# Sparse attention in front of a gated MLP: visits of four units over a DRAM image, filler matmuls in the front, a new order

## The chip, the core and the metric

One core of one Trainium2 chip runs the whole program. The metric is the device time of one execution in microseconds (us); the number given for a kernel is the median of its runs.

## What is computed

The program joins two operators. The first is attention over 8 batches x 8 heads, 576 positions and 64 values per head. Heads 0 to 3 let a query see its own position and the 31 before it; heads 4 to 7 let it see the earlier positions that leave the same remainder by 32. The second is a gated MLP on the 4608 x 512 result.

```python
scores = q @ k.T / sqrt(D)
rel = pos[:, None] - pos[None, :]
mask_local = (rel >= 0) & (rel < 32)                          # heads 0..3
mask_strided = (rel >= 0) & (pos[None] % 32 == pos[:, None] % 32)   # heads 4..7
attn = softmax(where(mask, scores, -1e9)) @ v                 # 8 x 8 x 576 x 64
x = attn.transpose(0, 2, 1, 3).reshape(4608, 512)
xn = x / sqrt(mean(x * x, axis=-1) + 1e-6) * rms_g
g = xn @ w_gate                                               # 512 -> 1536
out = (g * sigmoid(g) * (xn @ w_val)) @ w_out                 # 1536 -> 512
```

## The kernel before

The MLP works on nine chunks of 512 tokens. Each float32 product is made of three matmuls on rounded parts (high x high, low x high, high x low), and the program has 3528 matmuls of 128x512 for them; their lines are L1040, L1119, L1508, L1673, L1897 and L2099. Chunk 0 goes alone and the last two together in their own way (L1508, L1673); chunks 1 and 2 join for their output product (L1897), and chunks 3 to 6 go by pairs in a scheme that saves products (L2099, L1897).

The attention is cut into 96 units: a batch, a pair of heads (`p`; below 2 local, else strided) and a third of the queries (`j`). A unit has one or two tiles per head, of 96 queries (local) or of 108 to 126 queries (strided, by the table `RES`). There are two paths.

- **The old path** (units 0 to 19). Fifteen of these units form the front, which runs before the first large matmul; the others stand between the large matmuls of chunk 0. Steps: scores (in the front over zero-padded copies of the keys, L697, of all 128 rows; else over 64 rows, L701; a mask is added by a bf16 matmul, L691, in the front), row maximum on DVE, four exps on ACT (L728), normalization, transposes on PE with an identity (L796) and a copy (L800), values (L832). Squares and their sums for the RMS factor follow (L897, L902, L929, L948).
- **Visits** (units from `BT` = 20 on). `step_e` and `step_d` make one visit of two units. Scores are matmuls of 32x64 on the band alone (L587), DVE masks and takes the row maximum over 128 columns (L594), ACT makes the exps (L601), DVE the reciprocals (L619, L620), ACT or POOL the normalization (L631, L633). DVE transposes blocks of 32x32 over 1024 columns (L644). Three moves within SBUF of 32 KB each (L647) carry the blocks that belong to the next group of keys, and ACT or POOL clears the place they came from (L651, L653). At a later visit the values follow (L826).

The MLP's weights arrive in an eight-byte form; during chunk 0 ACT, DVE and POOL convert them (L2259 to L2281) and SP stores them to DRAM (L2285, L2288). The RMS factor of chunk 1 onwards is made by a column sum over all 128 partitions (L929 for chunk 1), a square root on ACT with its table load (L979) and four reciprocals on DVE (L982).

What sets the order: each operation is recorded in a `Plan` with an engine, a cost and what it reads and writes. The table `ORDER` (a packed list of numbers) then gives the sequence in which each of the five engines issues, and it is followed as it stands. A DMA issued by SP that must wait holds up all that is behind it on SP. Every instruction of PE that waits holds up PE.

## Time and profile before

| what | us |
|---|---|
| median of 3 runs (lowest, highest) | 949.84 (949.37, 953.02) |
| the profiled execution's own time | 951.61 |
| its span in the profile | 949.8 |
| PE busy / DVE busy / ACT busy / POOL busy | 925.6 / 771.4 / 624.4 / 308.5 |

The mean granted clock of PE in that execution is 0.998 of full speed. A matmul of float32 operands leaves two records in the profile, so "x48" in a timeline row of scores stands for 24 matmuls; a 128x512 matmul of the MLP leaves one. Matmuls overlap in the pipeline, so the price of one is read from start to start; its own duration is longer. "Idle before" is time in which an engine had nothing to do, with what released it.

### The profile page before, as it was taken

The numbers are of one execution on the slowest core, as the hardware profiler recorded it, in microseconds if no ns is written. First come the engines' busy times: TensorE is split into PE (matmuls) and PEld (weight loads), VectorE is DVE, ScalarE is ACT, GpSimd is POOL, SyncE is SP. The second block draws the span as 40 slices with busy tenths as digits, with TensorE's granted clock in tenths as the row PEclk, the third lists the DMA queues.
The fourth block names the chain that finished last, engine by engine and source line by source line (L and its number), as shares of the span: only waits on it lengthen the run. The fifth ranks groups of instructions, "written<-read, shape, count | busy, mean of one in ns | idle before, by whom it ended". The sixth has DMA issues, their size and how long they took to land.

```text
span 949.8 us, 18934 instructions
## 1 busy us (share of the span) xinstructions
PE 925.6 (97%) x6470; PEld 744.4 (78%) x6470; DVE 771.4 (81%) x1810; ACT 624.4 (66%) x1758; POOL 308.5 (32%) x294
## 2 busy tenths in 40 slices
PE   8999999999999899999999999999999999999998
PEld 7777766887788687788887778788888888888886
DVE  5899999978988999988768999755579995467891
ACT  7999996658786789776569786656377633333340
POOL 7334335336334322445212423201034310114130
PEclk9999999999999999999999999999999999999999
DMA  9999666664556677965765779684537794683561
GB/s 298 391 355 387 221 256 229 204 215 167 174 189 221 207 251 259 369 263 182 246 204 170 226 245 357 234 319 154 193 115 216 247 374 177 236 299 130 172 184 66
DMA packets 100928, 223.22 MB, mean 235 GB/s; under 512 B 11552, under 2 KB 34784, under 8 KB 100832
## 3 DMA queue, kind: packets, MB, share of 16 engines
q1 hardware_dynamic: 100064, 221.17, 67.3%
q8 instruction: 51, 0.84, 0.4%
q10 hardware_dynamic: 768, 0.85, 0.3%
q14 instruction: 45, 0.37, 0.1%
HBM read 171.05 MB, written 47.19 MB: 230 GB/s over the span
## 4 chain that ended last, share of the span: by engine, by line
PE 77%; DVE 9%; DMA 6%; ACT 5%; issue 1%; ACTq 0%; SPq 0%; DVEq 0%
PE acc L2099 10%; PE g L2099 6%; PE v L2099 6%; PE acc L1897 6%; PE v L1897 5%; PE g L1040 5%; PE g L1897 5%; PE v L1040 4%; PE acc L1040 4%; PE acc L1508 3%; PE v L1508 3%; PE g L1508 3%; PE acc L1119 2%; PE acc L826 2%; PE pair L587 2%; PE g L1673 2%
## 5 line engine op out<-in xcount | busy, mean ns | idle before, releaser
L1040 PE MATMUL g<-xh,wg 128*128 128x512 f32 x192 | 61.3, 399 | 1.9 <-DVE e L1056 1.4
L1040 PE MATMUL v<-xh,wv 128*128 128x512 f32 x184 | 58.8, 400 | 0.7 <-DVE e L1094 0.7
L601 ACT ACTIVATE pp<-pp,my 96x128 f32<-96x128 f32 (+2 forms) x146 | 56.6, 392 | 3.9 <-DVE my L594 3.9
L919 POOL TENSOR_TENSOR ssq<-ssq,srt 128x512 f32<-128x512 f32 x21 | 28.8, 1369 | 82.8 <-ACT srt L914 82.8
L601 ACT ACTIVATE pT<-pT,my 96x128 f32<-96x128 f32 (+2 forms) x130 | 50.4, 392 | 1.3 <-DVE my L594 1.2
L1040 PEld LDWEIGHTS g<-xh,wg 128*128 128x128 f32 x192 | 34.9, 188 | 11.4 <-DVE e L1056 2.3
L1040 PEld LDWEIGHTS v<-xh,wv 128*128 128x128 f32 x184 | 33.6, 188 | 9.4 <-DVE e L1094 1.0
L1040 PE MATMUL g<-xl,wg 128*128 128x512 f32 x96 | 37.6, 391 | 1.3 <-DVE xl L1015 1.3
L631 ACT ACTIVATE pp<-pp,my 96x128 f32<-96x128 f32 (+2 forms) x118 | 37.0, 391 | 1.2 <-DVE my L620 1.0
L879 ACT COPY raw<-acc 128x192 f32<-128x192 f32 (+16 forms) x97 | 22.2, 345 | 23.1 <-PE acc L826 21.0
L1040 PE MATMUL v<-xl,wv 128*128 128x512 f32 x92 | 36.1, 392 | 0.2 <-DVE xl L1015 0.2
L594 DVE CUSTOM_DVE_ANT_0 pp<-pair,cb 96x128 f32<-96x128 f32 (+2 forms) x146 | 33.1, 282 | 1.8 <-PE pair L587 1.7
L587 PEld LDWEIGHTS pair<-xx,xx 64*32 64x32 f32 (+2 forms) x1920 | 22.2, 105 | 14.9 <-issue 10.4
L651 ACT ACTIVATE pp<-pp 32x256 f32<-32x256 f32 x44 | 18.2, 415 | 23.7 <-DMA pp<-pp 23.1
L1040 PE MATMUL acc<-xh,wv 128*128 128x512 f32 x104 | 32.7, 395 | 0.8 <-DVE or L1086 0.8
L1119 PE MATMUL acc<-or,hh 128*128 128x512 f32 x96 | 30.8, 400 | 1.2 <-POOL or L2281 1.2
L631 ACT ACTIVATE pT<-pT,my 96x128 f32<-96x128 f32 (+2 forms) x96 | 30.0, 397 | 3.0 <-DVE my L620 3.0
L1040 PE MATMUL acc<-xh,wg 128*128 128x512 f32 x96 | 30.3, 397 | 0.3 <-DVE hl L1056 0.2
L594 DVE CUSTOM_DVE_ANT_0 pT<-pair,cb 96x128 f32<-96x128 f32 (+2 forms) x130 | 29.2, 282 | 0.6 <-PE pair L587 0.6
L587 PE MATMUL pair<-xx,xx 64*32 64x64 f32 (+1 forms) x1920 | 28.2, 221 | 1.2 <-DVE pair L579 1.0
L2099 PE MATMUL acc<-wg,wv 128*128 128x512 f32 x102 | 28.7, 390 | 0.0
L2099 PE MATMUL acc<-wv,wv 128*128 128x512 f32 x102 | 28.7, 389 | 0.0
(918 smaller groups left out, 3143.0 us busy)
## 6 DMA issues: line engine op xcount, KB each, us to landing
wv<-wsv SPq DMA_DIRECT2D x36, 512.0 KB, 8.0
wg<-wsg SPq DMA_DIRECT2D x26, 512.0 KB, 8.3
or<-tg SPq DMA_DIRECT2D x22, 512.0 KB, 6.4
th<-tg SPq DMA_DIRECT2D x21, 512.0 KB, 6.1
tl<-tg SPq DMA_DIRECT2D x21, 512.0 KB, 6.0
xx<-in_qT_dram SPq DMA_DIRECT2D x31, 288.0 KB, 5.5
wg<-wos SPq DMA_DIRECT2D x32, 256.0 KB, 3.7
xx<-in_kT_dram SPq DMA_DIRECT2D x28, 288.0 KB, 5.0
```

What stands on the lines that cost most here:

```text
L587: nc.tensor.matmul(out=singles[0][h][g:g + w, o:o + n], lhsT=qt[r, q0 + g:q0 + g + w], rhs=kt[r, k0 + g:k0 + g + n], start=True, stop=True)
L594: nc.vector.tensor_tensor_reduce(out=PX[x][:m, :, g0 + 2 * h + t], in0=sp[h][:, t], in1=mk[t], scale=-0.125, scalar=3.0e38, op0=ALU.add, o ...
L601: nc.scalar.activation(out=v, in_=v, func=AF.Exp, scale=-1.0, bias=mx2[z][:m, u, h, t:t + 1], accum_out=su2_[z][:m, u, h, t, 0:1])
L631: nc.scalar.activation(out=w, in_=w, func=AF.Copy, scale=mx2[z][:m_, y, h, t:t + 1])
L826: nc.tensor.matmul(out=po[64 * h:64 * h + 64, x * 32 * nx:(x + 1) * 32 * nx].rearrange("d (x q) -> d x q", q=32), lhsT=vt_of(vt, p)[:n, h, ...
L879: nc.scalar.copy(out=d, in_=s)
L919: op("Pool", pool(CH), at, lambda e: (nc.vector if e == "DVE" else nc.gpsimd).tensor_tensor(out=ssq, in0=ssq, in1=roots["srt"], op=ALU.add ...
L1040: nc.tensor.matmul(out=out, lhsT=wt[:, w, sl], rhs=xhl[x, kc], start=(kc == 0 and i == 0), stop=(kc == KC - 1 and i == 2))
L1119: nc.tensor.matmul(out=acc[t], lhsT=x[h][:, sl], rhs=wt[:, w], start=(u == 0 and i == 0), stop=(u == NU - 1 and i == 2))
L1508: nc.tensor.matmul(out=banks[bk], lhsT=w, rhs=X[a, k].tile(y), start=start and k == 0 and i == 0, stop=stop and k == 1 and i == 2, skip_gr ...
L1897: nc.tensor.matmul(out=banks[bks[j]], lhsT=w.tile(v, k, j), rhs=x.tile(k, y), start=start and n == 0 and i == 0, stop=stop and n == KT - 1 ...
L2099: nc.tensor.matmul(out=banks[bk], lhsT=w, rhs=xtile(a, k, y), start=start and k == 0 and i == 0, stop=stop and k == 1 and i == 2, skip_gro ...
```

## The change

1. Front. The keys of a unit arrive in one tile for both heads, without the zero-padded copies, and the scores use 64 rows (L707 after; 11 units move to it). The eight clears of 64x608 on POOL go. Three units (3, 6, 9) are "wide": one subtraction on DVE and one exp over all columns on ACT instead of four exps with their sums. Forty filler matmuls of 128x128 (L2258 after), whose result nobody reads, stand on PE in the front. The two warm-up matmuls of 128x512 (L402) stay, later in the order.
2. Visits have four units, that is two pairs, from unit 24 on; units 20 to 23 go to the old path, whose other form (`TP`) goes. Scores, masks, exps and normalization use a compact band of 64 columns; the block transpose covers 512 columns. The matmuls of scores fall from 960 to 912, the blocks of scores from 38 to 19. Runs of attention work between large matmuls fall from 68 to 57.
3. In place of the moves and clears a pair is written to one of two images in DRAM by two DMAs (L662 after, 96 or 128 KB each, 72 in all) and read back by one (L664, 384 or 512 KB, 36 in all). The read lays each block on its diagonal and brings zeros for the rest; `zeros()` clears both images once, with four DMAs of 256 KB at the start.
4. Chunk 1's RMS factor is made on columns, as chunk 0's is: four small matmuls, nine small operations on DVE, a spread by four 128x128 matmuls (L1001 after) and a copy take the place of one 128x512 float32 matmul, the square root and four reciprocals.
5. In the weights' conversion one ACT operation takes a constant instead of a bias tile, and 12 of 36 roundings go from ACT to DVE.
6. `ORDER` is new as a whole.

```diff
@@ constants
-RES = [7, 7, 6, 6, 6]
+RES = [7, 7, 7, 7, 4]
+RC = (1,)
+WIDE = (3, 6, 9)
+FILL = 40
+VIS = ((12, 12.0, 22, (28, 4, 4)), (22, 0.0, 45, (36, 4, 4, 4, 4, 4, 4)), (45, 0.0, 69, (60, 4, 4, 4, 4, 4, 4)), (69, 0.0, 90, (84, 4, 2, 2, 4)))
-BT = 20
-TP = 21
+BT = 24
+TP = 99
-RELX = {12: 0.0, 13: 36000.0, 14: 0.0, 15: 46000.0}
-RELD = {14: 37000.0, 15: 0.0}
+RELX = {}
+RELD = {}
...
@@ ORDER = (...): all of its lines are replaced
...
+    PC = [t[:, 0:CH].rearrange("q (c g k) -> q c g k", c=2, k=32) for t in qs_]
...
-    for x in range(NPB):
-        op("Pool", 1200, -1, lambda x=x: nc.gpsimd.memset(pq[x], 0.0), writes=[("pp", x)])
...
+    def zeros():
+        zz = tbufs[2]
+        op("Pool", 400, -1, lambda: nc.gpsimd.memset(zz, 0.0), writes=[("ts", 1, 1)])
+        for x in range(2):
+            for y in range(2):
+                op("SP", 430, 0, lambda x=x, y=y: nc.sync.dma_start(out=whole_[x][:, CH * y:CH * y + CH], in_=zz),
+                   reads=[("ts", 1, 1)], writes=[("im", x, y)], bytes_=P * 2048, rel=22000.0)
...
+        c0 = 128 * ((i - BT) % 4)
+        sp = [singles[0][h][:m, c0:c0 + 64 * nt].rearrange("q (t x k) -> q t x k", x=2, k=32) for h in range(2)]
+        mk = [cm[:m, 2 if p > 1 else 0 if j == 0 and t == 0 else 1] for t in range(nt)]
...
-            if i == BT:
-                nc.vector.memset(pair_, 0.0)
-            for t, tt_ in enumerate(tl):
-                q0, k0 = (PAD + LQ * tt_, LQ * tt_) if p < 2 else (PAD + NROW * RES0[tt_],) * 2
+            for t, tile_ in enumerate(tl):
+                q0, k0 = (PAD + LQ * tile_, LQ * tile_) if p < 2 else (PAD + NROW * RES0[tile_],) * 2
                 for g in range(0, m, 32):
-                    w, n = min(32, m - g), min(64, P - g)
+                    qe = min(g + 32, m)
                     for h in range(2):
                         r = slice(64 * h, 64 * h + 64)
-                        o = 256 * u + P * t + g
-                        nc.tensor.matmul(out=singles[0][h][g:g + w, o:o + n], lhsT=qt[r, q0 + g:q0 + g + w], rhs=kt[r, k0 + g:k0 + g + n],
-                                         start=True, stop=True)
+                        w = min(64, SW + 32 - k0 - g)
+                        for a, e, k in ((0, w, k0 + g), (w, 64, k0)):
+                            if e > a:
+                                nc.tensor.matmul(out=singles[0][h][g:qe, c0 + 64 * t + a:c0 + 64 * t + e], lhsT=qt[r, q0 + g:q0 + qe],
+                                                 rhs=kt[r, k:k + e - a], start=True, stop=True)
...
-        op("DVE", DVT + 2 * CH / 0.96, 0, lambda: nc.vector.transpose(out=qs_[x], in_=qs_[x]), reads=[], writes=[("pu", x, 0), ("pu", x, 1), ("pp", x)])
-        for y in range(3):
-            near, far = PX[x][32 * y:32 * y + 32, y + 1].rearrange("k g q -> k (g q)"), PX[x][32 * y + 32:32 * y + 64, y].rearrange("k g q -> k (g q)")
-            op("SP", SPMV, 0, lambda near=near, far=far: nc.sync.dma_start(out=far, in_=near), reads=[("pp", x)], writes=[("pd", x, y)], bytes_=32 * 1024)
-
-            def clear(e, near=near):
-                if e == "ACT":
-                    nc.scalar.activation(out=near, in_=near, func=AF.Copy, scale=0.0)
-                else:
-                    nc.gpsimd.memset(near, 0.0)
-            op(CLW[0][0], CLW[0][1], 0, clear, reads=[("pd", x, y)], writes=[("pz", x, y)], also=CLW[1:])
+        near, z = qs_[x][:, 0:CH], x % 2
+        op("DVE", DVT + CH / 0.96, 0, lambda: nc.vector.transpose(out=near, in_=near), reads=[], writes=[("pu", x, 0), ("pu", x, 1), ("pp", x)])
+        w = 3 if wus[i][1] < 2 and wus[i - 1][1] < 2 else 4
+        for c in range(2):
+            n = min(P - 32 * c, 32 * w)
+            op("SP", 600, 0, lambda c=c, n=n: nc.sync.dma_start(out=diag[z][c][0:n // 32], in_=near[0:n, 256 * c:256 * c + 256]),
+               reads=[("pp", x)], writes=[("im", z, c)], bytes_=n * 1024 + 1)
+        op("SP", 430, 0, lambda: nc.sync.dma_start(out=qs_[x][:, 0:256 * w], in_=whole_[z][:, 0:256 * w]), reads=[("im", z, 0), ("im", z, 1)],
+           writes=[("pp", x)], bytes_=P * 1024 * w + 1)
...
-                    if o < KZ:
-                        nc.tensor.matmul(out=sp[h][:, x], lhsT=qt[:, q0:q0 + m],
-                                         rhs=wraw[kz_key(o, h)].bitcast(F32)[:, k0:k0 + n], start=i >= PM,
-                                         stop=i >= PM or x == nt - 1)
-                    else:
-                        nc.tensor.matmul(out=sp[h][:, x], lhsT=qt[r, q0:q0 + m], rhs=kt[r, k0:k0 + n],
-                                         start=i >= PM, stop=i >= PM or x == nt - 1)
...
+        wide = i in WIDE
+
         def rowmax():
+            if wide:
+                for hs, pr in joint(pn):
+                    full = pr[:m, :, 0:nt * n].rearrange("q h (t k) -> q h t k", k=n)
+                    nc.vector.tensor_reduce(out=mx[:, hs], in_=full, axis=AX.X, op=ALU.max, negate=True)
+                    nc.vector.tensor_tensor(out=pv[:, hs], in0=full, in1=mx[:, hs].unsqueeze(3).broadcast_to([m, hs.stop - hs.start, nt, n]), op=ALU.add)
+                return
...
+            if wide:
+                e = buf[:m, 0:2 * nt * n]
+                nc.scalar.activation(out=e, in_=e, func=AF.Exp, scale=0.125)
+                return
...
+        if c in RC:
+            for t in range(4):
+                op("PE", 230, at, lambda t=t: nc.tensor.matmul(out=banks[bk][:, 0:4], lhsT=ssq[:, P * t:P * t + P], rhs=sel[:, 3 - t:7 - t],
+                                                               start=t == 0, stop=t == 3),
+                   reads=["sel", "ssq"], writes=[key] + alias.get(key, []) + ([("S", 0), ("T", 0)] if bk[0] == "b" else []))
...
+        if c not in RC:
+            op("ACT", act(CH) + 90, at, sqrt, reads=["eps", key], writes=["srt"], tab="sqrt")
+        for q in range(0, CH if c not in RC else 0, P):
...
+    for _ in range(FILL):
+        op("PE", 224 + SMD, 0, lambda: nc.tensor.matmul(out=bank["g"][:, 0:P], lhsT=ones, rhs=ebuf[:, 0:P], start=True, stop=True),
+           reads=["ones", "wz", "e"], writes=["g"])
...
-            nc.scalar.activation(out=lo32, in_=top, func=AF.Identity, scale=1.0 / 32, bias=low3)
-        op("ACT", 655, at, last3, reads=["low3"], writes=[wk])
+            nc.scalar.activation(out=lo32, in_=top, func=AF.Copy, scale=1.0 / 32, bias=-31.0 / 64)
+        op("ACT", 562, at, last3, writes=[wk])
...
```

The order shows it at three places. First, PE at the very start (`pair` and `acc` are PSUM, `wg`/`wv` hold the padded keys, `xx` the queries, `cb` the mask). Before:

```order
L402 MATMUL v<-e,ones 128x512 x2
L691 LDWEIGHTS hl_106
L691 MATMUL pair<-cb,hl_106 96x256
L691 LDWEIGHTS hl_106
L691 MATMUL pair<-cb,hl_106 96x256
L697 MATMUL pair<-wg_180,xx_82 96x128
L697 MATMUL pair<-wv_181,xx_82 96x128
L697 MATMUL pair<-wg_180,xx_82 96x128
L697 MATMUL pair<-wv_181,xx_82 96x128
```

After:

```order
L2258 MATMUL g<-e,ones 128x128 x16
L702 LDWEIGHTS hl_109
L702 MATMUL pair<-cb,hl_109 96x256
L702 LDWEIGHTS hl_109
L702 MATMUL pair<-cb,hl_109 96x256
L707 MATMUL pair<-wg_187,xx_83 96x128 x4
L2258 MATMUL g<-e,ones 128x128 x2
```

The warm-up is replaced by sixteen fillers, and the other 24 stand in groups of one to three further on. Second, PE around a visit (`pp` and `pT` hold a pair's weights, `vt` the values of v). Before, among the products of L1897:

```order
L587 MATMUL pair<-xx_83,xx_82 32x64 x6
L587 MATMUL pair<-xx_83,xx_82 12x32 x2
L587 MATMUL pair<-xx_85,xx_84 32x64 x6
L587 MATMUL pair<-xx_85,xx_84 30x32 x2
L587 MATMUL pair<-xx_85,xx_84 32x64 x6
L587 MATMUL pair<-xx_85,xx_84 30x32 x2
L826 MATMUL acc_70<-pp_97,vt_88 64x96 x8
L826 MATMUL acc_70<-pp_98,vt_87 64x128 x8
L1897 MATMUL acc_72<-wg_3961,wg_3613 128x512 x3
L1897 MATMUL acc_72<-wv_3948,wg_3613 128x512 x3
L1897 MATMUL acc_72<-th_3955,wv_3645 128x512 x3
L1897 MATMUL g<-wg_3320,wg_3700 128x512 x3
```

After:

```order
L600 MATMUL pair<-xx_86,xx_85 32x64 x24
L600 MATMUL pair<-xx_84,xx_83 32x64 x6
L600 MATMUL pair<-xx_84,xx_83 30x64 x2
L600 MATMUL pair<-xx_84,xx_83 32x64 x6
L600 MATMUL pair<-xx_84,xx_83 30x64 x2
L600 MATMUL pair<-xx_84,xx_83 32x64 x6
L600 MATMUL pair<-xx_84,xx_83 30x64 x2
L600 MATMUL pair<-xx_84,xx_83 32x64 x6
L600 MATMUL pair<-xx_84,xx_83 30x64 x2
L850 MATMUL acc_71<-pp_98,vt_88 64x96 x8
L850 MATMUL acc_71<-pp_99,vt_88 64x96 x4
L850 MATMUL acc_71<-pp_99,vt_89 64x96 x4
```

A visit now makes the scores of four units in one run and the values of others behind them. Third, SP around the moves. Before:

```order
L647 DMA pT_99<-pT_99 32x256 x3
L2285 DMA wsv_151<-wv_1845 128x1024
L1309 DMA or_1875<-wos_116 128x2x256
L2288 DMA wos_126<-or_1867 256x1x256 x2
L2288 DMA wos_127<-or_1824 256x1x256 x2
L1309 DMA or_1875<-wos_117 128x2x256
L647 DMA pT_100<-pT_100 32x256 x3
L1303 DMA tt<-wos_116 128x2x256
L1273 DMA tg_157<-th_1924 128x1024
L1273 DMA tg_157<-tl_1935 128x1024
```

After:

```order
L662 DMA im_104<-pp_99 3x32x256
L662 DMA im_104<-pp_99 4x32x256
L1353 DMA or_2387<-wos_124 128x2x256
L1315 DMA to_197<-th_1918 512x1x256
L662 DMA im_103<-pp_98 4x32x256
L662 DMA im_103<-pp_98 3x32x256
L1315 DMA to_197<-tl_1927 512x1x256
L664 DMA pp_99<-im_104 128x1024
L664 DMA pp_98<-im_103 128x1024
L1317 DMA tg_155<-th_1918 128x1024
L1317 DMA tg_155<-tl_1927 128x1024
L542 DMA xx_83<-in_qT_dram 128x576
```

Instead of three moves behind one transpose there are two writes for each pair and then a read which waits for them. Between the last write of the second image and its read two other DMAs are issued here.

## Rows read from the trace of the kernel before

**Rows 1.** Busy time by engine on the page: us, share of the span, instructions.

```profile
PE 925.6 (97%) x6470; PEld 744.4 (78%) x6470; DVE 771.4 (81%) x1810; ACT 624.4 (66%) x1758; POOL 308.5 (32%) x294
```

**Rows 2.** Stretches of the span: from:to and length, then the busy us of PE, PE's weight loads, DVE, ACT and POOL, PE's granted clock, the DMA engines' busy share and GB/s. The last row is a part of the fifth stretch.

```profile
0.00:34.00 34.00, 29.22 (x263) 23.39 (x263) 21.93 (x78) 27.06 (x116) 23.23 (x50) 1.00 0.96 333
34.00:126.00 92.00, 90.45 (x663) 71.06 (x662) 85.15 (x232) 90.63 (x246) 33.36 (x30) 1.00 0.89 331
126.00:176.00 50.00, 45.44 (x363) 33.99 (x362) 48.24 (x105) 38.08 (x97) 21.45 (x17) 1.00 0.61 215
176.00:320.00 144.00, 141.29 (x1252) 112.77 (x1251) 127.22 (x347) 103.73 (x341) 68.04 (x67) 1.00 0.58 197
320.00:332.00 12.00, 9.41 (x95) 6.96 (x96) 11.10 (x46) 8.13 (x37) 1.11 (x1) 0.86 0.67 211
332.00:700.00 368.00, 363.73 (x2693) 293.71 (x2692) 294.61 (x705) 255.29 (x736) 101.58 (x89) 1.00 0.70 239
700.00:946.00 246.00, 245.81 (x1152) 202.57 (x1150) 182.68 (x300) 101.13 (x193) 59.68 (x43) 1.00 0.61 208
326.00:328.00 2.00, 2.00 (x23) 1.16 (x29) 2.00 (x6) 2.00 (x10) 0.00 (x0) 0.50 0.81 288
```

**Rows 3.** Timeline of one pair of a visit in chunk 1: start, duration, engine. The pair is `pT`: scores of its first unit, transpose, moves, values.

```profile
208.68 0.69 PE L587 MATMUL pair<-xx,xx 64*32 64x64 f32 x48
...
215.91 1.25 DVE L644 STREAM_TRANSPOSE pT<-pT 128x1024 f32<-128x1024 f32 x1
...
217.18 1.84 SPq L647 DMA_DIRECT2D pT<-pT  x3
...
222.82 0.88 PE L826 MATMUL acc<-pT,vt 108*64 108x128 f32 x12
```

**Rows 4.** Timeline of PE in the front and up to the first large matmul: start, duration until the last record ends, line.

```profile
1.52 3.77 PE L402 MATMUL v<-e,ones 128*128 128x512 f32 x4 [1.52 <-DVE onesr L392]
5.10 0.41 PE L691 MATMUL pair<-cb,hl 96*96 96x256 bf16 x2
5.34 0.38 PE L697 MATMUL pair<-wg,xx 128*96 128x128 f32 x2
...
6.22 0.38 PE L691 MATMUL acc<-cb,hl 96*96 96x256 bf16 x2
...
29.83 0.68 PE L701 MATMUL pair<-xx,xx 64*96 64x128 f32 x8
30.44 0.59 PE L832 MATMUL acc<-xl,vt 108*64 108x108 f32 x8
...
33.95 0.72 PE L1040 MATMUL g<-xh,wg 128*128 128x512 f32 x2
```

**Rows 5.** PE by line and form: busy us of all, mean ns of one record.

```profile
L902 PE MATMUL v<-few,ssq 128*128 128x4 f32 x16 | 2.0, 249 | 0.0
```

**Rows 6.** Timeline of PE around two blocks of scores, of 48 and of 64 records.

```profile
101.25 0.63 PE L1040 MATMUL g<-xh,wg 128*128 128x512 f32 x2
101.71 0.39 PE L1040 MATMUL g<-xl,wg 128*128 128x512 f32 x1
102.03 0.69 PE L587 MATMUL pair<-xx,xx 64*32 64x64 f32 x48
102.65 0.73 PE L1040 MATMUL v<-xh,wv 128*128 128x512 f32 x2
103.22 0.40 PE L1040 MATMUL v<-xl,wv 128*128 128x512 f32 x1
...
175.20 0.82 PE L587 MATMUL pair<-xx,xx 64*32 64x64 f32 x64
175.95 0.74 PE L1040 MATMUL acc<-xh,wv 128*128 128x512 f32 x2
```

**Rows 7.** Busy time of single lines in a stretch (PE, PE's weight loads): L701, L796 and L832 in 34 to 180 us, then L587 and L826 in 180 to 946 us.

```profile
34.00:180.00 146.00, 4.06 (x48) 2.84 (x48) 1.00 0.80 292
34.00:180.00 146.00, 4.67 (x36) 3.81 (x34) 1.00 0.80 292
34.00:180.00 146.00, 5.54 (x84) 3.95 (x84) 1.00 0.80 292
180.00:946.00 766.00, 23.78 (x1616) 18.70 (x1616) 1.00 0.65 220
180.00:946.00 766.00, 29.44 (x496) 23.94 (x496) 1.00 0.65 220
```

**Rows 8.** Waits of PE: who waited, for what, total us, times, longest.

```profile
PE acc L1119 <- POOL or L2281: 1.2, 1, 1.2
```

**Rows 9.** DVE by line and form: busy us of all, mean ns of one, idle time before.

```profile
L982 DVE RECIPROCAL srt<-srt 128x128 f32<-128x128 f32 x28 | 25.2, 925 | 0.7 <-ACT srt L979 0.7
```

**Rows 10.** Timeline of PE at the longest wait.

```profile
325.42 1.18 PE L1897 MATMUL v<-wg,wg 128*128 128x512 f32 x3 [2.59 <-DVE wv L1086]
```

**Rows 11.** DMA issues: count, KB each, median us from issue to landing.

```profile
th<-tg SPq DMA_DIRECT2D x21, 512.0 KB, 6.1
...
vt<-in_vl_dram SPq DMA_DIRECT2D x16, 384.0 KB, 4.9
...
wos<-or SPq DMA_DIRECT2D x24, 256.0 KB, 3.6
...
pp<-pp SPq DMA_DIRECT2D x60, 32.0 KB, 3.4
```

294 lines of the change are left out of this document (162 added, 132 removed).

## The prediction

> **What bounds the kernel now.** I read the page's busy times first: PE works 925.6 us of a span of 949.8 [rows 1]. The large matmuls are the same 3528 before and after, so only two things can move the time: what PE does beside them, and its idle time. Next I cut the span into stretches [rows 2]. Length less PE's busy time gives the idle time of each: 4.8 us in the front (0 to 34), 1.6 in 34 to 126, 4.6 in 126 to 176, 2.7 in 176 to 320, 2.6 in 320 to 332, 4.3 in 332 to 700, 0.2 in 700 to 946. That is 20.6, and some 3.8 follow as the tail. The reader should look at the other engines in the same rows. From 34 to 126 ACT is busy 90.6 of 92, and DVE 85.2. From 126 to 176 DVE is busy 48.2 of 50, from 320 to 332 it is 11.1 of 12: where PE waits, DVE is full. The single waits agree: the longest, 2.59, is for DVE (L1086) [rows 10], another, 1.2, for the weights' conversion (L2281) [rows 8].
>
> The profiled execution took 951.6, which is its span and 1.8 around it; that is 1.8 above the median of 949.84. The sum is made against 951.6 and then lowered by 1.8.
>
> **The front, part by part.** Four matmuls of 128 columns take from 5.34 to 6.22, so 0.22 each [rows 4]. Forty fillers: 40 x 0.22 = +8.8 of PE time. The warm-ups' four records took 1.52 to 5.10, 0.90 each [rows 4], where a record of 128 columns takes 0.11 and one of 512 would take 0.44: they ran at the lower of the clock's two levels. The first 16 fillers take that place, so I let 8 of them cost 0.44: +1.8 (lower end 0, if the clock rises sooner; upper end 3.5, all 16). The warm-ups stand later and then take 1.8 and not 3.6: -1.8. The scores of 11 units go from L697, 0.88 a unit (5.34 to 6.22), to the 64-row form, which took 0.61 (29.83 to 30.44) [rows 4]: 11 x 0.27 = -3.0. Four more small matmuls of sums, at most 0.25 each by their busy time [rows 5]: +1.0. Front: **+6.8** of PE work.
>
> **Between the large matmuls.** A block of 48 score records takes 0.62 from its start to the next large matmul, one of 64 takes 0.75 [rows 6]. So a record costs 0.008 and a block 0.23 besides. Nineteen blocks fewer: -4.4; 48 matmuls (96 records) fewer: -0.8. Around a run of attention work the last large matmul stands 0.32 (101.71 to 102.03), and the first two after it 0.57 (102.65 to 103.22) where two take 0.46 elsewhere (101.25 to 101.71, [rows 6]); with 0.23 for one, a run costs 0.20. Eleven runs fewer: -2.2. Four units (20 to 23) change path. In a visit a unit takes 23.78/64 + 29.44/68 = 0.80 of PE; on the old path, at 8, 4 and 8 records a unit, 4.06/6 + 4.67/9 + 5.54/10.5 = 1.72 [rows 7]. So 4 x 0.92 = +3.7. Chunk 1's factor: two records of 512 columns go (-0.9), four small matmuls at 0.25 and four of 128 columns at 0.22 come (+1.9): +1.0. Sum: **-2.7**. PE's work in all: +4.1.
>
> **The idle time.** DVE is full where PE waits, and the change takes work from it: 38 transposes of 1.25 [rows 3] become 36 of half the columns, some 24 us less over the span; row maxima and exps cover half the columns; four reciprocals at 0.925 [rows 9] leave the stretch from 126 to 176. ACT and POOL lose the clears. Against that stand 12 roundings more on DVE in chunk 0, where its 85 of 92 leaves 7, and nine tiny operations. I take: front -2.5 of its 3.3 after the start, because fillers and not waits then stand there; 126 to 176 -3.5 of 4.6, because DVE has 3.7 less there and PE comes later; 320 to 332 -2.2 of 2.6; the three other stretches -2.2 of 8.5. New waits at visits: +1.0. Sum **-9.4**. No row shows how the new order fits, so this is the softest term: at worst only the front's 2.5 goes, at best some 16.
>
> **The trip through DRAM.** A pair now makes two writes and then a read that waits for them. A write lies between a move of 32 KB, 3.4, and a store of 256 KB, 3.6; a read of 384 to 512 KB between 4.9 and 6.1 [rows 11]. So the trip takes 8.3 to 9.7 behind the transpose, where the three moves took from 217.18 to the values at 222.82, 5.6 [rows 3]. PE does not wait for it as long as the values are asked for at a later visit. The read holds SP too: one issue is 1.84/3 = 0.6 [rows 3], so a read behind its second write stands up to 3.6 - 2 x 0.6 = 2.4. Queued behind it are loads for the MLP and the next queries (the third place of the order); they take 6.1 to land [rows 11], and a lead shorter than that plus 2.4 turns into a wait of PE. I count both in the +1.0. The Trainium skill, page "DMA: Bandwidth & Descriptors", section "Anatomy of one DMA", speaks against such a trip: most of a fixed cost of about 2 us is the receipt of the last byte, and that is heaviest with HBM as target. By its figure two DMAs would cost about 4 us and the bytes (an estimate from that page), less than the rows give; the +1.0 would be nearer 0 and the forecast 943.5.
>
> The four clears of the images (1 MB in all) add some 3 us of DMA at the 333 GB/s of the front, where the share is 0.96 [rows 2]. PE's other work and the fillers cover them; without that cover they cost up to 3.
>
> **Sum.** 951.6 + 4.1 - 9.4 = 946.3; less 1.8 it is **944.5**, or 0.6% faster. About 0.5%, 4.75 us, is what a measurement of this kernel can tell from no change: faster is below 945.1, slower above 954.6.
>
> **Rivals.**
> - *The idle time moves and does not go* (0.13). PE's wait is then at another place of the same full engines. For it: in 34 to 126 ACT is full and PE hardly waits, so PE and ACT already keep step, and roundings move to DVE. Only the front's 2.5 goes: 951.6 + 4.1 - 2.5 - 1.8 = 951.4.
> - *The trip ends later than the next visit: slower* (0.19). The second pair of a visit starts its maxima behind the first pair's. Before, a pair needed 14 us from its scores to its values (208.68 to 222.82, [rows 3]). Add the trip's 3 to 4 more and a second pair's 3 or so, less half a transpose: 20, and up to 25 where DVE is full, in 126 to 176 and 320 to 332 [rows 2]. Visits in the densest chunks lie 84 to 99 large matmuls apart by the order, at 0.23 some 19 to 23, and with the block itself 22 to 25. So it decides at about 23. If 8 visits wait 1.5 each: +12. For one such wait the rows show what follows: a clock of 0.50 in 326 to 328, after 2.59 of idle time [rows 2, 10]. 944.5 + 12 = 956.5, say 957.
> - *Fillers stand only where PE would wait* (0.18). Then they cost only what they fill in the front, 4.5 less than counted, and the lighter DVE halves the remaining waits, some 5 more: 935.
> - *The clock falls in the front* (0.04). The 64-row matmuls and fillers in ones to threes leave PE with pauses behind them; what one pause did is in [rows 2, 10]. Ten us of front at the lower level hold 5 us of work: 944.5 + 5 = 949.5. The Trainium skill, page "TensorE: Matmul & The Clock Gate", Part 1, has the throttled state as the default and activity as what releases it; the 0.90 for a warm-up record agrees with that.
>
> **How the numbers follow.** My own case has 0.46 and reaches from 940 to 949; its middle lies just inside "faster", so 0.27 of it counts there and 0.19 as no change. Faster: 0.27 + 0.18 = 0.45. Same: 0.19 + 0.13 + 0.04 = 0.36. Slower: 0.19. The range from 931 to 958 takes in every case but the outer ends of the second and third rival.
>
> **What would show it.** Right: the first large matmul at 37 to 39 and not at 33.95; fillers at 0.22; PE busy about 930; idle time in 126 to 176 near 1; score blocks of 0.8 to 1.2 that need no wait; reads of the image done well before the values that use them. Wrong: waits of PE for the image's read (the second rival); PE idle unchanged outside the front (the first); large matmuls before 36 (the third); a granted clock below 1.00 in the front after 6 us (the fourth).

## The result, and the profile after

The changed kernel took 964.24 us (median of 4 runs, 961.37 to 965.68), the kernel before in the same session 950.69. The ratio is 1.0134, with a 95% interval of 1.011 to 1.0158. So the change is **slower by 1.3%**: 19.7 above the forecast of 944.5, and above the range. The profiled execution took 964.97, its span 962.8. Below, medians and ratios leave out three executions set apart as slow: 980.47 of a_nofill, 1528.79 of o_halfwait and 1343.35 of the kernel before.

Busy time by engine on the page after, to be set beside [rows 1]:

```profile
PE 934.9 (97%) x6504; PEld 755.8 (79%) x6504; DVE 764.4 (79%) x1849; ACT 530.9 (55%) x1552; POOL 328.9 (34%) x284
```

The reader should see that PE works 9.3 us longer where 4.1 was forecast, and that DVE and ACT did become lighter (ACT by 93.5, DVE by 7.0 only: the transposes alone were forecast at 24 less). Length less PE's busy time gives PE's idle time: 27.9 us after, 24.2 before. It should have fallen by 9.4.

The same stretches as in [rows 2], of the kernel after; the last two rows are parts of the second and the sixth:

```profile
0.00:34.00 34.00, 32.40 (x302) 25.96 (x302) 22.83 (x74) 24.06 (x90) 14.85 (x38) 1.00 0.91 328
34.00:126.00 92.00, 88.40 (x528) 67.40 (x530) 84.57 (x218) 77.79 (x217) 43.12 (x31) 0.96 0.87 320
126.00:176.00 50.00, 48.22 (x324) 38.59 (x321) 46.30 (x109) 29.44 (x87) 27.31 (x22) 1.00 0.71 234
176.00:320.00 144.00, 139.48 (x1316) 113.51 (x1314) 113.71 (x373) 77.89 (x299) 57.77 (x54) 1.00 0.70 227
320.00:332.00 12.00, 10.91 (x159) 8.11 (x161) 10.04 (x15) 3.95 (x6) 6.81 (x6) 1.00 0.83 263
332.00:700.00 368.00, 356.51 (x2723) 288.74 (x2718) 285.31 (x766) 221.64 (x690) 116.26 (x92) 0.99 0.80 276
700.00:946.00 246.00, 245.89 (x1109) 202.99 (x1108) 198.08 (x295) 95.37 (x170) 62.82 (x44) 1.00 0.64 217
40.00:42.00 2.00, 2.00 (x6) 1.32 (x4) 1.97 (x6) 1.88 (x12) 0.00 (x0) 0.50 0.80 313
368.00:370.00 2.00, 2.00 (x6) 1.61 (x5) 1.99 (x4) 1.53 (x7) 0.64 (x2) 0.50 1.04 409
```

From 126 to 176 the idle time fell from 4.6 to 1.8 and from 320 to 332 from 2.6 to 1.1, the direction forecast. From 176 to 320 it rose from 2.7 to 4.5, and from 332 to 700 from 4.3 to 11.5. There the DMA engines' share rose too, from 0.58 to 0.70 and from 0.70 to 0.80. The granted clock is at the lower level, 0.50, in four stretches of some 4 us: 39.5 to 43, 53 to 57, 367 to 371 and 446 to 450. Before there was one. The first two are there without the trip as well (0.50 from 40 to 42, 0.53 from 54 to 56); the last two follow PE's waits of 2.3 and 3.1, at 367 and 446, and are not there without it.

A stretch doesn't hold the same work in two kernels. The large matmuls are the same 3528 in all, so progress is best read by their number. These are the starts of the n-th (us), from the timelines of PE; the last column is an experiment without the trip through DRAM, told below:

| n-th large matmul | before | after | after less before | no trip less before |
|---|---|---|---|---|
| 0 | 33.95 | 39.49 | +5.5 | +5.5 |
| 150 | 83.59 | 95.04 | +11.5 | +11.2 |
| 450 | 168.66 | 180.54 | +11.9 | +11.7 |
| 1050 | 338.08 | 345.24 | +7.2 | -1.8 |
| 1200 | 379.37 | 392.18 | +12.8 | -0.9 |
| 1500 | 457.54 | 476.71 | +19.2 | -0.4 |
| 1800 | 537.37 | 551.33 | +14.0 | -5.6 |
| last | 945.84 | 958.66 | +12.8 | -6.6 |

The two versions of the change run alike up to the 450th. Between the 450th and the 1500th the changed kernel loses 19.4 us against the one without the trip, and from there on nothing more.

The waits of PE after (who waited, for what, total us, times, longest), beside [rows 8] and the 2.59 of [rows 10]:

```profile
PE g L2143 <- DVE or L2193: 3.1, 1, 3.1
PE v L1084 <- DVE or L1130: 2.6, 1, 2.6
PE acc L1941 <- DMA wv<-to: 2.3, 1, 2.3
PE acc L1001 <- DVE few L995: 2.1, 1, 2.1
PE g L1941 <- DMA or<-to: 1.6, 1, 1.6
PE acc L1941 <- DMA xh<-wos: 1.5, 2, 1.4
...
PE acc L850 <- DMA pp<-im: 1.4, 2, 1.0
```

PE hardly waits for the image itself (`pp<-im`, the only row of it, 1.4 us in 2 times). It waits for loads of the MLP (`wv<-to`, `or<-to`, `xh<-wos`). Before, PE's longest wait for any DMA was 0.9. The two longest waits are for DVE; without the trip the first is 0.6 and the second is not there. The waits of SP, the queue that issues the image's transfers and the loads, show the trip:

```profile
SPq L664 <- DMA im<-pp: 37.2, 15, 6.1
SPq L664 <- DMA im<-pT: 35.1, 17, 3.9
```

L664 is the read of the image, which waits for the pair's two writes: 72.3 us in 32 waits, of 36 reads. SP issues in order, so whatever stands behind such a read stands too, as SP's timeline shows for two reads:

```profile
379.56 3.77 SPq L664 DMA_DIRECT2D pp<-im  x2
383.37 0.42 SPq L1866 DMA_DIRECT2D or<-to  x1
```

These sums do not yet tell a loss: SP's waits of all kinds add up to some 630 us before, 638 after and 665 without the trip, most of them for PE. A hold costs only where it makes a needed transfer late. The chain of waits around one of them (start, us, what):

```profile
375.65 7.29 DMA im<-pp
...
383.00 6.29 DMA pp<-im
...
389.35 10.39 DMA out_dram<-tt
...
399.80 7.61 DMA or<-to
...
407.45 0.99 PE g L1941 x3
...
457.09 6.69 DMA im<-pp
...
463.80 5.53 DMA pp<-im
```

The read starts as the write lands (7.29 after its issue, where [rows 11] had 3.4 and 3.6 for transfers of about that size), a store of the MLP as the read lands, a load as the store lands, and PE then waits 1.6 for that load. SP is not stopped all that time: from 383.37 to 388.09 it issues seven other transfers. From 390 to 410 the DMA engines are busy all the time (share 1.02), as they were before (1.02 and 1.03). A second trip stands on the chain at 457. The chain after consists of DMA to 14% of the span, and of PE to 66% (6% and 77% before).

PE's timeline of the front after, to be set beside [rows 4]:

```profile
1.47 5.65 PE L2258 MATMUL g<-e,ones 128*128 128x128 f32 x32 [1.47 <-DVE few L403]
...
10.31 0.94 PE L2258 MATMUL g<-e,ones 128*128 128x128 f32 x6
11.09 0.38 PE L702 MATMUL pair<-cb,hl 96*96 96x256 bf16 x2
...
39.05 0.79 PE L2258 MATMUL g<-e,ones 128*128 128x128 f32 x4
39.49 1.20 PE L1084 MATMUL g<-xh,wg 128*128 128x512 f32 x2
...
43.14 0.73 PE L1084 MATMUL g<-xh,wg 128*128 128x512 f32 x2
```

The first large matmul starts at 39.49. It takes 1.20 where the same pair takes 0.73 at 43.14: the clock is at its lower level from there to 43, though PE had no pause of more than 0.25 since the first filler.

### The profile page after: what moved, and what is told of

It reads as the page before. It is cut to its first block, busy times and chain, and to the rows that moved or that the text cites. A ratio compares the mean times of both kernels' runs of the same rounds, so it can differ in the third digit from the quotient of the medians.

```text
span 962.8 us, 18783 instructions
## 1 busy us (share of the span) xinstructions
PE 934.9 (97%) x6504; PEld 755.8 (79%) x6504; DVE 764.4 (79%) x1849; ACT 530.9 (55%) x1552; POOL 328.9 (34%) x284
## 4 chain that ended last, share of the span: by engine, by line
PE 66%; DMA 14%; DVE 11%; ACT 5%; issue 2%; POOL 1%; SPq 0%; DVEq 0%; POOLq 0%
PE acc L2143 8%; PE g L2143 6%; PE acc L1941 6%; PE v L2143 6%; PE v L1941 4%; PE g L1941 4%; PE acc L1552 3%; PE v L1552 3%; PE g L1552 3%; PE acc L1084 3%; PE g L1084 3%; PE v L1084 2%; PE acc L850 2%; PE acc L1717 2%; PE pair L1552 2%
## 5 line engine op out<-in xcount | busy, mean ns | idle before, releaser
L614 ACT ACTIVATE pT<-pT,my 96x64 f32<-96x64 f32 (+2 forms) x134 | 44.7, 339 | 5.1 <-DVE my L607 5.1
L614 ACT ACTIVATE pp<-pp,my 96x64 f32<-96x64 f32 (+2 forms) x130 | 43.3, 338 | 7.5 <-DVE my L607 7.0
L903 ACT COPY raw<-acc 128x192 f32<-128x192 f32 (+13 forms) x80 | 18.9, 328 | 28.9 <-PE acc L850 21.9
L2198 POOL TENSOR_TENSOR wg<-or,or 128x512 f32<-128x512 f32 x6 | 8.2, 1366 | 68.9 <-DVE or L2174 46.7
L2143 PE MATMUL acc<-wg,wv 128*128 128x512 f32 x102 | 29.2, 394 | 0.0
L1219 DVE TENSOR_TENSOR tt<-tt 128x256 f32<-128x256 f32 (+1 forms) x43 | 24.4, 578 | 4.5 <-POOL tt L1355 3.6
L761 POOL TENSOR_TENSOR pp<-pp,mx 126x504 f32<-126x504 f32 (+2 forms) x15 | 20.9, 1396 | 17.4 <-PE g L1084 4.3
L2161 ACT ACTIVATE or<-g 128x512 f32<-128x512 f32 x24 | 14.3, 596 | 22.1 <-PE g L2143 16.7
L614 ACT ACTIVATION_READ_ACCUMULATOR pT<-pT,my 96x1 f32 (+2 forms) x134 | 25.7, 192 | 0.0
L600 PEld LDWEIGHTS pair<-xx,xx 64*32 64x32 f32 (+2 forms) x1824 | 19.9, 104 | 6.6 <-issue 6.6
L1098 ACT ACTIVATE e<-g 128x512 f32<-128x512 f32 x24 | 14.2, 592 | 19.6 <-PE g L1084 18.4
```

Source lines behind the costliest of these rows:

```text
L600: nc.tensor.matmul(out=singles[0][h][g:qe, c0 + 64 * t + a:c0 + 64 * t + e], lhsT=qt[r, q0 + g:q0 + qe], rhs=kt[r, k:k + e - a], start=Tru ...
L614: nc.scalar.activation(out=v, in_=v, func=AF.Exp, scale=-1.0, bias=mx2[z][:m, u, h, t:t + 1], accum_out=su2_[z][:m, u, h, t, 0:1])
L761: (nc.vector if e == "DVE" else nc.gpsimd).tensor_tensor(out=pv, in0=pv, in1=mx.unsqueeze(3).broadcast_to([m, 2, nt, n]), op=ALU.mult)
L1219: elementwise(width, lambda e: both(e).tensor_tensor(out=dst(), in0=a(), in1=b(), op=ALU.subtract), [], keys)
L2143: nc.tensor.matmul(out=banks[bk], lhsT=w, rhs=xtile(a, k, y), start=start and k == 0 and i == 0, stop=stop and k == 1 and i == 2, skip_gro ...
```

## The experiments

Each is the changed kernel with one edit. Medians are in us, ratios are to the kernel before of the same session (949.5 to 950.6 in the five sessions), with the 95% interval.

**The trip left out, whole and by halves.** First both directions:

```diff
-            op("SP", 600, 0, lambda c=c, n=n: nc.sync.dma_start(out=diag[z][c][0:n // 32], in_=near[0:n, 256 * c:256 * c + 256]),
+            op("SP", 600, 0, lambda c=c, n=n: None,
...
-        op("SP", 430, 0, lambda: nc.sync.dma_start(out=qs_[x][:, 0:256 * w], in_=whole_[z][:, 0:256 * w]), ...
+        first = i - BT < 2 * NQ
+        op("SP", 430, 0, lambda: nc.sync.dma_start(out=qs_[x], in_=whole_[z]) if first else None, ...
```

> The changed kernel with all writes to the image and all but the first read of each buffer left out: the values multiply the transposed blocks where they lie, so the attention's result is another one. Theory TRIP: the waits of PE for transfers (wv<-to 2.3, or<-to 1.6, xh<-wos 1.5, image 1.4) and the 3.1 for DVE at 445 us, with the two stretches of half clock behind them, go; the total falls by 8 to 12, to 952 to 956. Theory FRONT: the trip is hidden and the total falls by less than 4.

It took 945.33, ratio 0.9948 [0.9928, 0.9968]. Without the trip the rest of the change is faster than before. The trip costs 964.24 - 945.33 = 18.9; the two were run in different sessions, and by the ratios it is 17.7. The stretch in which it was lost, in the kernel without it:

```profile
332.00:700.00 368.00, 364.94 (x2758) 296.87 (x2756) 294.36 (x752) 225.46 (x681) 117.65 (x93) 1.00 0.70 240
```

PE's idle time there is 3.1, where it was 11.5 with the trip, and the clock is 1.00. By the spans, 962.8 and 943.4, the trip's 19.4 are 13.0 of idle time and 6.4 of longer work (PE 934.9 against 928.5).

Then the writes alone left out (g_nowrite: only the first edit above; the reads bring zeros), and the later reads alone (h_noread: only the second).

> The changed kernel with the writes to the images left out and all reads kept, from images that only the clearing has written (the attention's result is another one). Nothing is left of the trip but the reads' bytes and issues. Leaving out all of it gave 945.3, a read that did not wait 958.8, the change 964.2. If the bytes of the reads (15.6 MB) make the 13.5 us that the free read left, this stays at 955 to 959; if it is the writes (7.9 MB in pieces of 1 KB), it falls to 945 to 950.

> The changed kernel with all writes to the images kept and only the first read of each buffer (the attention's result is another one). If the reads' bytes and their wait on SP are the loss, 945 to 949; if the writes are, 955 to 959; if it takes both for the transfers to be late, both this and the kernel without writes stand near 948 to 952.

Reads without writes: 944.39, 0.9949 [0.9933, 0.9966]. All the bytes of the reads cost nothing when they wait for no write. Writes without reads: 950.05, 1.0000 [0.9986, 1.0013], so the writes cost 4.7. PE's wait of 2.6 for DVE (L1130) goes with them: with the writes alone it is 2.2, and without the writes, or without the trip, it is not there. The two halves alone do not add up to 18.9; the rest needs both.

**The wait and the size, apart.** The read was first taken from a third image that only the clearing writes (c_readfree), so that it should wait for nothing:

```diff
+    still = dp.tile([1, 4 * DG], F32, name="still")[0, 0:P * 1024].rearrange("(p e) -> p e", e=1024)
...
-        ... out=qs_[x][:, 0:256 * w], in_=whole_[z][:, 0:256 * w]
+        ... out=qs_[x][:, 0:256 * w], in_=still[:, 0:256 * w]
```

> The changed kernel with every image read taken from a third, cleared image that no pair is written to: same bytes and same issues, but the read no longer waits for the writes, so SP is not held by it (the result of the attention is another one). Before, the reads held SP for 72 us in 32 waits. If the hold is what makes the loads behind it late, the total falls nearly as far as without the trip, by 6 to 10; if the bytes do it (DMA share 0.80 instead of 0.70 between 332 and 700 us), by less than 3.

It took 958.79, 1.0086 [1.0057, 1.0115]. The edit did not do what it was meant to: SP's waits were still there,

```profile
SPq L665 <- DMA im<-pp: 35.7, 15, 6.1
SPq L665 <- DMA im<-pT: 35.5, 18, 4.2
```

since the read overwrites the buffer that the writes are still reading. With the same bytes and the same waits (71.2 against 72.3 us) it is still 5.5 faster than the change (4.6 by the ratios); the two differ only in where the read takes its bytes, and why that helps was not followed. So two versions read only columns 512 and on, which the writes don't touch: from the image, with the wait (o_halfwait), and from the unwritten one, without it (n_halffree).

```diff
-        ... out=qs_[x][:, 0:256 * w], in_=whole_[z][:, 0:256 * w]
+        ... out=qs_[x][:, CH:256 * w], in_=whole_[z][:, CH:256 * w]      (o_halfwait)
+        ... out=qs_[x][:, CH:256 * w], in_=still[:, CH:256 * w]          (n_halffree)
```

> The changed kernel with each image read cut to the columns from 512 on (128 or 256 KB instead of 384 or 512), which keeps its wait for the pair's writes; the attention's result is another one. Leaving the writes out gave 944.4 though all bytes of the reads stayed, leaving the reads out 950.0, and the read from a cleared image 958.8: that read still overwrote the columns the writes read and so still waited (71 us on SP). If the wait on SP is the loss, halving the bytes changes little: 958 to 964. If bytes are, it falls to 953 to 957.

> The same cut read, but from a cleared image that no pair is written to, into columns that no write reads: the same bytes and issues as its companion and no wait for the writes. If the wait on SP is the loss, this gives 948 to 952 (as without reads, 950.0), some 10 us below its companion; if the bytes are, the two stand within 3 us of each other.

With the wait: 955.50, 1.0050 [1.0031, 1.0068]. Without: 950.63, 1.0001 [0.9981, 1.0021]. Both move the same bytes; SP's waits differ, first with:

```profile
SPq L664 <- DMA im<-pp: 34.7, 16, 6.1
SPq L664 <- DMA im<-pT: 31.8, 19, 3.6
```

and then without:

```profile
SPq L665 <- DMA im<-pT: 1.8, 3, 0.9
SPq L665 <- DMA im<-pp: 0.6, 1, 0.6
```

So holding SP costs at most 4.9 by itself (the source of the read differs as well), with 66.5 us of waits in all (in the profiled execution, which at 950.60 was the shortest of its nine), and the bytes of the half read cost 0.6 above the writes alone. Next the read was cut to 8 columns with its wait kept (r_tinywait), and, the other way, the bytes were to be brought back without a wait, as two pieces (q_dblfree):

```diff
+        nc.sync.dma_start(out=qs_[x][:, CH:2 * CH if first else CH + 8], in_=whole_[z][:, CH:2 * CH if first else CH + 8])   (r_tinywait)
...
+            nc.sync.dma_start(out=qs_[x][:, CH:2 * CH], in_=still[:, CH:2 * CH])     (q_dblfree, twice for w == 4)
```

> The changed kernel with writes kept and each image read cut to eight columns (4 KB), which still waits on SP for the pair's writes (the first read of each buffer has 512 columns). The wait without bytes. Half a read without the wait gave 950.6, with it 955.7. If the wait alone is the 5 us, this gives 954 to 957; if the wait hurts only because a large read lands late behind it, it stays at 949 to 952.

> The changed kernel with writes kept and the read made of two pieces from a cleared image, into columns that no write reads: as many bytes as the change reads (384 or 512 KB a pair), no wait for the writes. One half of it gave 950.6. If bytes beside the writes are what costs, this rises to 955 to 959; if only a read that waits costs, it stays at 949 to 953.

The tiny read took 953.40, 1.0042 [1.0028, 1.0056]: 3.4 above the writes alone, with 70.3 us of waits on SP. The two pieces took 1028.03, 1.0823 [1.0791, 1.0856], and don't answer their question: they go to the same columns, so each second piece waited on SP for the first.

```profile
SPq L670 <- DMA pT<-still: 43.8, 9, 7.0
SPq L668 <- DMA pT<-still: 41.8, 9, 8.6
SPq L668 <- DMA pp<-still: 41.5, 9, 6.3
SPq L670 <- DMA pp<-still: 40.3, 9, 7.2
```

Nor do they price a hold: 95 us more of them than in the changed kernel (167.4 against 72.3) came with 64 us more of time, but PE waited 51.9 for the pieces themselves.

The ladder, as medians: no trip 945.3; writes 950.0 (+4.7); a tiny read that waits 953.4 (+3.4); half of the read 955.5 (+2.1); the whole 964.2 (+8.7). They are from different sessions; by the ratios the steps are 4.9, 4.0, 0.8 and 8.0. SP's waits for the image are nearly the same on the last three (70.3, 66.5 and 72.3 us), so it is not the length of the hold that tells them apart. Nor is it the size alone: the whole read of c_readfree, which waits as long (71.2), stands at 958.8.

**The wait put elsewhere.** If a hold of SP is the trouble, the trip may be issued by another engine, or later. Reads issued by ACT (d_readact), writes issued by ACT (s_writeact), both by POOL (m_pooltrip), reads moved on SP behind the next four transfers (i_later):

```diff
-        ... nc.sync.dma_start(out=qs_[x][:, 0:256 * w], ...
+        ... nc.scalar.dma_start(out=qs_[x][:, 0:256 * w], ...                      (d_readact)
...
-        ... nc.sync.dma_start(out=diag[z][c][0:n // 32], ...
+        ... nc.scalar.dma_start(out=diag[z][c][0:n // 32], ...                     (s_writeact)
+        ... nc.gpsimd.dma_start(...                              (m_pooltrip, both places)
...
+        for i in self.late:                                                        (i_later)
+            a = b = next(k for k, x in enumerate(out) if x[0] == i)
+            step = 0
+            while step < 4 and i not in self.ops[out[b + 1][0]][1]:
+                b += 1
+                step += out[b][1] == "SP"
+            out.insert(b, out.pop(a))
```

> The changed kernel with the image reads issued by ACT at the same place of the order: the wait for the writes holds ACT and no longer SP. If the hold of SP is the loss, the total falls by 3 to 8, less than without any wait because ACT is held instead (its exps stand behind); if the bytes are, it stays within 3 us or rises with the held ACT.

> The changed kernel with the two writes of each pair issued by ACT instead of SP, reads as they are. SP no longer waits for DVE's transposes (59 us of waits in the run without reads, whose 950.0 is 4.7 above the run without any trip), and the writes do not stand behind SP's loads. If these two are part of the loss, 955 to 960. Rival: ACT waits for the transposes instead, its exps and copies come late, as with the reads on ACT (973): 966 or more.

> The changed kernel with the writes to the image and the reads issued by POOL instead of SP, at the same places of the order. SP then waits neither for transposes nor for the image. POOL is busy 329 of 963 us, so if its own work has room for the waits, the time falls to 946 to 952; rival: POOL's issues and waits (108 transfers, some 3 us each) delay the subtractions and sums that DVE and PE wait for, and the time stays above 960, as it rose to 973 with the reads on ACT.

> The changed kernel with each image read moved behind the next four transfers of SP's order (as far as nothing depends on it), everything else kept. If the wait that a read makes on SP is worth 5.5 us (964.2 to 958.8 with a read that need not wait), and not the bytes, this gives 958 to 961, unless a later read makes the values late: then PE waits for the image and it stays at 964 or above.

They took 972.97 (1.025 [1.0219, 1.0282]), 986.95 (1.0395 [1.0355, 1.0436]), 1155.33 (1.2155 [1.2117, 1.2193]) and 1023.6 (1.0765 [1.0732, 1.0799]). All are worse than on SP at once. With writes on ACT, PE waits for ACT's own work behind them:

```profile
PE g L2143 <- ACT hh L1948: 10.3, 2, 10.0
```

With the reads later, PE waits for the image:

```profile
PE acc L859 <- DMA pT<-im: 24.4, 9, 10.0
PE acc L859 <- DMA pp<-im: 21.9, 6, 5.7
```

By the timelines after, the second pair of a visit mostly has 4 to 8 us from its read's issue to the visit's values, not much more than the read takes to land (5.53 and 6.29 on the chain). A theory that the read may simply be issued later falls with it.

**The trip replaced by moves inside SBUF** (k_sbmoves: 6 or 7 moves of 32 KB a pair into two wide buffers):

```diff
+            def move(c=c, n=n):
+                ...
+                for y in range(n // 32):
+                    nc.sync.dma_start(out=dq[z][32 * (y + c):32 * (y + c) + 32, 256 * y:256 * y + 256],
+                                      in_=near[32 * y:32 * y + 32, 256 * c:256 * c + 256])
```

> The changed kernel with the trip through DRAM replaced by moves within SBUF at the place of the writes: a pair's two halves of 256 columns go straight to their blocks in one of two wide buffers that is cleared once and keeps its zeros; six or seven moves of 32 KB a pair instead of two writes and a read, no image. If the trip's bytes and the read's wait are the loss, the time falls to 945 to 951, since 8 MB move instead of 23 and nothing on SP waits for a transfer. Rival: seven issues of 0.6 us hold SP as long as the waiting read did (4.2 us a pair against some 4), then it stays above 956.

It moves blocks into buffers that other steps still use, so part of the attention's result is another one. It took 978.19, 1.0302 [1.027, 1.0333]: twice as many issues and two buffers for four are no cure.

**The front.** Without fillers (a_nofill), and with the first 16 alone (p_fill16):

```diff
-    for _ in range(FILL):
-        op("PE", 224 + SMD, 0, lambda: nc.tensor.matmul(out=bank["g"][:, 0:P], ...),
+        op("PE", 224 + SMD, 0, lambda: None,                                       (a_nofill)
+    for k in range(FILL):
+        op("PE", 224 + SMD, 0, lambda k=k: nc.tensor.matmul(...) if k < 16 else None,   (p_fill16)
```

> The changed kernel (964 us) with its forty filler matmuls left out, the order otherwise kept. Theory FRONT (the fillers are PE time that the front did not have to spare: the first large matmul stands at 39.5 us instead of 33.95, and PE was idle only 1.9 us before it): without them the first large matmul comes 5 to 8.8 us earlier, the total falls to 955 to 960. Theory TRIP (the loss is made by the trip through DRAM between the large matmuls 1050 and 1500): whatever the front gains is mostly given back as waits for ACT and DVE in chunk 0, the total stays within 3 us of 964. Rival on the clock: without fillers the granted clock falls to 0.5 in the front as well, and the first large matmul comes hardly earlier.

> The changed kernel with the first sixteen filler matmuls and without the other 24. If the sixteen raise the clock and the front's own matmuls hold it, the first large matmul comes up to 5.3 us (24 x 0.22) before 39.5 and the total falls to 959 to 962. If the 24 are needed, the clock falls somewhere in the front, matmuls there last nearly twice as long, and the time is 964 to 973.

Without: 971.72 (961.56 to 974.72), 1.0202 [1.0133, 1.0272]. That interval and the change's own (1.0110 to 1.0158) overlap, so it is unclear whether the total is longer. Its profile is of the execution of 980.47, so it shows the place and not the size. There PE waits 5.26 for the mask, the first large matmul starts at 47.88 and not at 39.49, and PE's records in the front read:

```profile
5.26 0.66 PE L702 MATMUL pair<-cb,hl 96*96 96x256 bf16 x2 [5.26 <-DMA hl<-in_consts_dram]
5.85 1.17 PE L707 MATMUL pair<-wg,xx 64*96 64x128 f32 x8
```

where with the fillers the same forms take 0.38 and 0.68. With 16 fillers: 962.32, 1.0130 [1.0094, 1.0166], and the first large matmul at 46.66. Its stretches, in the columns of [rows 2]:

```profile
12.00:16.00 4.00, 3.39 (x30) 2.56 (x28) 3.34 (x11) 3.73 (x19) 2.65 (x3) 0.75 1.04 409
16.00:20.00 4.00, 4.00 (x28) 2.82 (x26) 2.34 (x10) 2.30 (x14) 2.50 (x3) 0.50 1.01 382
...
24.00:28.00 4.00, 4.00 (x34) 3.08 (x32) 1.61 (x6) 2.34 (x10) 1.82 (x2) 0.50 0.14 22
```

The clock falls between 12 and 16, after pauses of 0.66, 0.40 and 0.22 us at 11 to 14, and stays down though PE then has no idle time. The front is 7 us longer and yet the kernel takes 962: the time is made good between the 900th and the 1500th large matmul (476.00 there against 476.71). So in the profiled executions the fillers kept the clock up in the front, but they do not decide the 13.5 us.

The wait for DVE's root at 52 (`PE acc L1001`, 2.1) stands before the half clock from 53 to 57. In l_root that root goes four places ahead in the order:

```diff
             out.append(self.ops[i][0][ENGINES[code[2 * n + k]]][2])
+        out.insert(286, out.pop(290))
```

> The changed kernel with one move in DVE's order: the nine small operations of chunk 0's RMS factor stand before, not behind, a subtraction of the weights' conversion that took 1.78 us (48.0 to 49.7). PE's wait of 2.1 us at 52 us falls to some 0.3; if the stretch of half clock behind it (54 to 57 us, granted clock 0.50 in 54 to 56) follows from that wait, it goes too: 964 less 3 to 4, 960 to 961. If the half clock comes from the sparse matmuls of that stretch, only 1.8 is won.

The profile has no half clock at 53 to 57, and the 300th large matmul starts at 135.55, 2.9 earlier. The time is 962.57, 1.0142 [1.0109, 1.0176]: within the interval of the change, so a gain did not show at the end. Nor is the half clock shown to follow from that wait: o_halfwait, whose order there is the change's, has the same wait of 2.1 and a clock of 1.00 from 54 to 56.

**What might mend it.** The last runs joined what had helped: l_root and a read cut to 320 to 384 KB in two transfers (t_lessread), and that with the writes on ACT (u_allthree).

```diff
+                nc.sync.dma_start(out=qs_[x][:, 0:CH], in_=whole_[z][:, 0:CH])
+                nc.sync.dma_start(out=qs_[x][64:P, CH:256 * w], in_=whole_[z][64:P, CH:256 * w])
```

> The changed kernel with the read after the first use of a buffer cut to what has to be renewed: columns 0 to 511 of all rows and the rest of rows 64 to 127 alone, 384 and 320 KB instead of 512 and 384, in two transfers; and chunk 0's factor ahead on DVE (which alone gave 962.6). Halving the read to 256 and 128 KB had given 8.5 us. If the size of the waiting read is the loss, a quarter less gives 2 to 4: 958 to 961. If the second issue and its place eat it, 962 to 965.

> Both edits of the two companions together with the factor moved ahead. If both parts of the loss come back, 950 to 956, level with the kernel before; by the rival on ACT, 965 or more.

They took 960.33 (1.0099 [1.0071, 1.0126]) and 982.23 (1.0341 [1.0306, 1.0375]). The smaller read is 2.2 below l_root, which the two intervals do not tell apart; writes on ACT lose again. No version with the same result beat the kernel before.

## Why the prediction was wrong

**The step that failed** is the trip through DRAM: "a lead shorter than that plus 2.4 turns into a wait of PE. I count both in the +1.0." It measured 18.9 (17.7 by the ratios). The hold of SP was sized about right: up to 2.4 a read was forecast, and it is 72.3/32 = 2.3 in the mean, 6.1 at the longest. A write was put at 3.4 to 3.6, and the three on the chain took 7.29, 6.69 and 4.76; a read was put at 4.9 to 6.1, and the two took 6.29 and 5.53. What failed is the overlap: I took all of this as hidden, but for +1.0, behind the leads of the loads and of the values; I had the sentence about the loads' leads, and gave it no row. The runs show in its place 4.7 for the writes, 3.4 for reads that wait and carry hardly any bytes, and 10.8 more as the waiting read grows to its whole size and takes it from the image; the last part is measured, and its mechanism is open (below). To multiply the number of reads by the hold would not have given it either: nearly the same sum of waits went with 3.4 above the writes in one kernel and with 14.2 in the other.

The Trainium skill, page "DMA: Bandwidth & Descriptors", section "Anatomy of one DMA", gives about 2 us of fixed cost a transfer. The section is on transfers issued by GpSimd, and these are issued by SP. The five transfers of the trip on the chain took 4.76 to 7.29, their bytes included, and by the page the step would have missed by more.

**The rivals.** The second, a trip that ends later than the next visit, came nearest in time (957), but its mechanism is not what happened: PE waited 1.4 for the image. The waits that came are mostly for the trip's neighbours on the queue and for DVE. The first is right that idle time moved (it fell from 126 to 176 and rose from 332 to 700) and that PE's longest waits, 3.1 and 2.6, are for DVE; but without the trip they are 0.6 and none, so a full DVE alone does not make them. The third is wrong: the first large matmul is at 39.49. The fourth came in part, not in the front but at its end (39.5 to 43) and at 53 to 57.

**What was right.** Without the trip, the sum can be checked term by term. Idle time of PE up to the last large matmul went from 20.6 to 11.1, -9.5; forecast -9.4, or -10.4 without the +1.0 that stood for the trip. PE's work rose by 928.5 - 925.6 = 2.9; forecast +4.1. The time was 945.3; forecast 944.5, or 943.5 without the trip. That two sums agree doesn't make each term right, and some of the agreement is luck: in the front of the changed kernel PE had 37.6 us of work up to the first large matmul instead of 29.2, +8.4 and not +6.8, and 2.9 less of idle time (forecast 2.5). Of the 1.6, some 1.2 are the 24 later fillers, which took 0.27 each from start to start (three from 10.31 to 11.09) and not 0.22. The first large matmul came 5.5 later (forecast 4.3); "37 to 39" was too early. From 126 to 176 the idle time fell by 2.8 (forecast 3.5).

**What stays open.** The size of a read that waits. Its bytes cost nothing when it does not wait (944.4 with all reads and no writes, 950.6 with half reads and writes), but when it does, the step from the half to the whole costs 8.7. Size is not all of that: the whole read of c_readfree, with the same waits, is 3.3 above the half, and 5.5 come only when it is taken from the image that was just written. The chain at 383 to 407 suggests that transfers behind it wait until it has landed. But SP's waits for transfers other than the image's add up to 35 us without the trip, 47 with the tiny read, 50 with the half and 54 with the whole, and also to 50 with the writes alone (950.0) and to 57 in the kernel before (950); so this is argued and not shown. A rival is the DMA engines' own capacity: from 380 to 410 their share is 0.94, 1.02 and 1.02 after and 1.01, 1.03 and 0.60 without the trip, so a hold or more bytes just there may not be made up. A whole read free of any wait, beside writes, was not run: it needs a buffer that the writes don't read from. Nor is it shown why the clock falls at 39.5; the profiled executions of o_halfwait and l_root have 1.00 from 40 to 42, with the same front.

## What to carry to other kernels

A transfer that waits on an engine that issues in order also delays what stands behind it. Look at what that is, and how long its lead is, before looking at who reads the data; the sum of the holds is not the price (some 70 us of them cost 3.4 here with a tiny read and 14.2 with a whole one). Moving such a wait to another engine moves the bill, since that engine has a queue as well. When a step is replaced by one with a chain of two transfers, leave each half out first: here the two halves cost 4.7 and nothing, and the rest came only when the reads waited for the writes, most of it when they were large.

## What the chip showed that I had not expected

- Fillers that do no work went with a shorter front, in one profiled execution each: the first large matmul is at 39.49 with 40 of them, at 46.66 with 16 and at 47.88 with none. Without them the same records took 1.7 times as long (0.66 against 0.38 and 1.17 against 0.68). The granted clock column shows 1.00 there all the same; that the clock is at its lower level there is read from the durations alone.
- PE busy 4.00 of 4.00 us at a granted clock of 0.50, for 12 us (16 to 28 of p_fill16), on the front's small matmuls after short pauses. A full busy column says nothing of the clock. The Trainium skill, page "TensorE: Matmul & The Clock Gate", Part 1, has the throttled state as the default and activity as what releases it; these rows show 12 us of a full busy column without a release.
- Issuing the same 108 transfers from POOL and not from SP cost 191 us.
